# A fused attention and two-MLP kernel: weight operands combined on VectorE a step ahead, later stream loads, deferred results in pieces

## The chip, the cores and the metric

One core of one Trainium2 chip runs the whole program. The metric is the device time of one execution in microseconds. TensorE (PE) multiplies matrices, ScalarE (ACT), VectorE (DVE) and GpSimd (POOL) work elementwise, and SyncE (SP) only issues transfers. Each engine works through its own instructions in their order and waits at each for what that one needs.

## The reference

Attention in two steps (32 packed queries per head attend to 576 keys, then the 576 queries attend to the packed result), an RMS norm with a gated MLP (512 to 1536 to 512), and a second MLP (512 to 2048 to 512) with a leaky activation, in float32 for 4608 tokens.

```
p_packed = sm_attn(p, k, v)
x = sm_attn(q, p_packed, p_packed)              # 8 x 8 heads x 576 x 64 -> 4608 x 512
xn = x / rms * rms_g
x = (silu(xn @ w_gate) * (xn @ w_val)) @ w_out  # 512 -> 1536 -> 512
h = x @ w_in
out = (max(h, 0) + alpha * min(h, 0)) @ w_out2  # 512 -> 2048 -> 512
```

## The kernel before, in words

Every float32 product is made of three products of halves: an operand is split into a high half on ScalarE (`split_hi`, L110) and the rest as a low half by a subtraction (`split_lo` on VectorE, L113), and `mm3` (L122 to L124) multiplies high by high, high by low and low by high.

**Stage one** does the attention and the gated MLP in 12 chunks of 320 or 512 tokens (`CH`, the loop over it begins at L938). A chunk has 12 steps `f`; a step multiplies into the two input banks, makes `s` (tanh on ScalarE, two VectorE operations), splits it, and multiplies the result of the step before by a block of `w_out`. Beside it, the generator `conv_late` prepares the weights of the second MLP in chunks 1 to 10. The last chunk (320 tokens) has no attention beside it; there `prep` makes the operands of the first pair of stage two, and `making` (below) its output weights.

**Stage two** is the second MLP, seven products in place of eight (the Winograd form of Strassen's scheme) for a two by two split, in five pairs of token blocks (`PAIRS`: 512, 512, 512, 384, 384 tokens each half). A pair has a loop over `i` = 0 to 7 and then 40 later blocks (`LATER`). An iteration of the loop makes seven products of a weight block with an operand half (`prod`, six matmuls each) into three PSUM banks `a`, `b_`, `c_`; VectorE adds them up (`m1` copied by ScalarE at L1224, then `u2`, `u3`, `h22`, `h12`, `h21`, `s1`, `s2`, `s3`), ScalarE and VectorE do the leaky activation (`halves_of`, `prelu`), and two output blocks of an earlier iteration are put between (`fill`). The product `prod(b_, 6)` writes on in the bank that `u2` reads, so it waits for `u2`.

**Weight operands.** Each weight needs seven combined blocks per `i`; `sevenths` makes them from four blocks of 128 x 256: `product` splits one (high on ScalarE, low on GpSimd at L288) into a buffer named `w7o` of which there are two, and SP stores it to `w7_dram` or `o7_dram`; `combine` (L292, GpSimd) adds or subtracts blocks in place. A set is made in four steps with 2, 1, 1 and 3 products and the sums between them. For the input weights the steps run in stage one, for the output weights in `make_o7`: a step that loads a 512 KB block (`o_raw`, L276), then the four steps. `next(making)` is called once per `f` in the last chunk and five times per iteration of the first pair (`make(pr)`).

**Stream.** All 560 combined blocks are read back in order of use into 12 buffers (`load_next`, L926): one load at each `f` of the last chunk, then one after each block's use. A load waits for its buffer's last reader, and every transfer in SP's row behind it waits too.

Of the kernel before, what the change touches and what calls it, by code (L numbers as in the profile page):

```python
# [18 lines left out]
def attention_moe_moe2_kernel(ctx, tc, q, k, v, p, w_gate, w_val, w_out, rms_g, w_in2, w_out2, alpha, out):  # L19
    nc = tc.nc  # L20
# [105 lines left out]
    with tc.manual_schedule():  # L126
# [146 lines left out]
        def make_o7():  # L273
            for i in range(NP2):
                t = one.tile([128, 2, 512], F32, tag="w64", name="o2_raw", bufs=NST)
                nc.sync.dma_start(out=t, in_=w_dram[i])  # L276
                yield
                yield from sevenths("o2", i, [t[:, e] for e in range(2)])

        def sevenths(kind, i, pair):  # L280
# [4 lines left out]
            def product(n, src):  # L285
                t = one.tile([128, 2, 256], F32R, tag="w7o", name="w7o", bufs=2)
                split_hi(t[:, 0], src)
                nc.gpsimd.tensor_tensor(out=t[:, 1], in0=src, in1=t[:, 0].bitcast(F32), op=ALU.subtract)  # L288
                nc.sync.dma_start(out=kept[i * 7 + n], in_=t.bitcast(F32))
# [4 lines left out]
            product(0, b11)  # L294
            product(3 if kind == "i2" else 2, b22)
            yield
            if kind == "i2":
                product(1, b12)
                combine(b22, b21, b22, ALU.add)
                yield  # L300
                combine(b21, b11, b21)
                product(4, b22)
                combine(b11, b22, b11)
                yield
                product(6, b21)
                combine(b12, b12, b11)
                product(5, b11)
                product(2, b12)
            else:
                product(1, b21)  # L310
                combine(b11, b12, b11)
                yield
                combine(b12, b22, b12)
                product(4, b11)
# [583 lines left out]
        LATER = [(x, n, i) for x, n in (("b", 5), ("c", 2), ("b", 6), ("d", 3), ("a", 1)) for i in range(NP2)]  # L898
        LAG = 2

        def all_blocks():
            q = [None, None]
            for pr in range(len(PAIRS)):
                for i in range(NP2):
# [4 lines left out]
                    q += [("o", i, 0), ("o", i, 4)]  # L909
# [28 lines left out]
        for c, (t0, n, cuts) in enumerate(CH):  # L938
# [100 lines left out]
            for f in range(NF):  # L1039
# [9 lines left out]
                if last:  # L1049
# [9 lines left out]
                    load_next()  # L1059
# [111 lines left out]

        acc = {}

        def make(pr):
            if pr == 0:
# [30 lines left out]
        for pr, (t0, w) in enumerate(PAIRS):  # L1206
            final = pr + 1 == len(PAIRS)
            late_h, waiting = {}, []
            for i in range(NP2):
# [10 lines left out]
                make(pr)  # L1220
# [10 lines left out]
                make(pr)  # L1231
# [11 lines left out]
                make(pr)  # L1243
# [4 lines left out]
                for _ in block("a", 0, i, g11, w, i == 0, i == NP2 - 1):  # L1248
# [3 lines left out]
                make(pr)  # L1252
# [10 lines left out]
                make(pr)  # L1263
# [5 lines left out]
            for f_ in waiting:  # L1269
                f_()  # L1270
            m1s, m5s, u2s, u3s = {}, {}, {}, {}

            def copies(to, x, w=w):
                for j, m in pieces(w):
                    to[j] = temp(m)
                    evac(to[j], banks(x, j)[:, 0:m], True)

            def sums(to, x, m1s=m1s, w=w):
                for j, m in pieces(w):
                    to[j] = temp(m)  # L1280
                    add2(to[j], m1s[j], banks(x, j)[:, 0:m])

            def results(r0, half, put, w=w, end=False):
                stg = one.tile([128, TPC, 256], F32, tag="w64", name="stg2", bufs=NST)
                rows = out[r0:r0 + w, half * 256:(half + 1) * 256].rearrange("(n p) d -> p n d", p=128)
                for j, m in pieces(w):
                    put(stg.rearrange("p n d -> p (n d)")[:, j * T:j * T + m], j, m)
                    n = m // 256
                    if end:
                        nc.sync.dma_start(out=rows[:, 2 * j:2 * j + n], in_=stg[:, 2 * j:2 * j + n])  # L1290
                if not end:
                    nc.sync.dma_start(out=rows, in_=stg[:, 0:w // 128])

            def done_a(final, t0=t0, w=w):
                results(t0, 0, lambda o, j, m: evac(o, banks("a", j)[:, 0:m], j == 0 or not final), w, final)
# [88 lines left out]
```

## Time and profile before

| | us |
|---|---|
| median of 3 runs | 1734.27 (1730.31 to 1735.71) |
| profiled execution | 1731.16 |
| its span | 1729.4 |
| busy: TensorE, VectorE, ScalarE, GpSimd | 1594.4, 1143.1, 898.7, 345.8 |

The profiled execution's time is its span and 1.8 us around it. Busy time of TensorE is not TensorE at its best rate: matmuls overlap, and the clock granted to it changes. The stretch from about 880 to 1070 us is the one in which the page's slices show TensorE at 5 to 8 tenths with the clock under full; everywhere else after the start it is at 9.

### The profile page before, as it was taken

The page shows a single profiled execution, that of the slowest core. Times are in us where ns is not written, and L with a number is a line of the kernel's source. Part 1 is how long each engine was busy: PE and PEld are TensorE (multiplying, and loading weights), DVE is VectorE, ACT ScalarE, POOL GpSimd, SP SyncE. Part 2 cuts the span into 40 slices and gives each one's busy share as a digit, 9 for nine tenths or more (in the row PEclk, how much of TensorE's full clock was granted, in tenths as well). Part 3 has the DMA queues.
Part 4 walks back from the last instruction along what each step waited for, and adds up shares of the span by engine and source line. Part 5 has one row for each costly group of instructions (what it writes and reads, how often), then busy time and mean ns, then how long its engine had stood idle before and what let it go on. Part 6 is the DMA issues. An engine that isn't in the chain of part 4 may idle for free.

```text
span 1729.4 us, 32037 instructions
## 1 busy us (share of the span) xinstructions
PE 1594.4 (92%) x11786; PEld 1397.7 (81%) x11786; DVE 1143.1 (66%) x2132; ACT 898.7 (52%) x1906; POOL 345.8 (20%) x350
## 2 busy tenths in 40 slices
PE   7789999999999999999988557999999999999999
PEld 5457887887878878788877446898899889999999
DVE  4786656656566565666445445877787778688776
ACT  4556455554555544555444334545565555555554
POOL 1441243334343412122123332000000000000000
PEclk8899999999999999999999878999999999999999
DMA  9876555546655656645355666576767667888876
GB/s 241 253 240 203 152 175 169 136 125 187 188 162 178 189 176 214 228 151 193 107 205 209 209 205 221 172 245 204 214 206 223 191 199 225 256 265 258 264 230 199
DMA packets 233884, 348.95 MB, mean 202 GB/s; under 512 B 62848, under 2 KB 96640, under 8 KB 233728
## 3 DMA queue, kind: packets, MB, share of 16 engines
q1 hardware_dynamic: 233728, 346.90, 64.8%
q8 instruction: 94, 1.54, 0.4%
q14 instruction: 62, 0.51, 0.1%
HBM read 284.96 MB, written 61.87 MB: 201 GB/s over the span
## 4 chain that ended last, share of the span: by engine, by line
PE 62%; DVE 12%; issue 8%; DMA 7%; ACT 6%; POOL 4%; SPq 1%; POOLq 0%; ACTq 0%; DVEq 0%
PE ps_g L122 10%; PE ps_g L123 10%; PE ps_g L124 10%; PE ps_y L122 7%; PE ps_y L124 7%; PE ps_y L123 6%; DMA o_raw<-w_dram 3%; PE ps_wg L744 2%; DVE hl L113 2%; POOL w7o L288 2%; PE ps_v L122 2%; PE ps_v L123 2%; PE ps_v L124 2%; DMA o_dram<-w7o 1%; DVE kept L1148 1%
## 5 line engine op out<-in xcount | busy, mean ns | idle before, releaser
L122 PE MATMUL ps_g<-yh,w 128*128 128x512 f32 (+1 forms) x560 | 211.6, 378 | 49.1 <-DVE tmp L1145 49.1
L122 PE MATMUL ps_y<-hh,in_h 128*128 128x320 f32 (+1 forms) x576 | 209.4, 364 | 13.9 <-ACT hh L110 13.9
L123 PE MATMUL ps_g<-yl,w 128*128 128x512 f32 (+1 forms) x560 | 209.7, 375 | 0.0
L124 PE MATMUL ps_g<-yh,w 128*128 128x512 f32 (+1 forms) x560 | 208.7, 373 | 0.0
L123 PE MATMUL ps_y<-hl,in_h 128*128 128x320 f32 (+1 forms) x576 | 199.0, 345 | 3.8 <-DVE hl L113 3.0
L124 PE MATMUL ps_y<-hh,in_l 128*128 128x320 f32 (+1 forms) x576 | 197.6, 343 | 1.5 <-DMA in_l<-lo_dram 1.5
L1068 DVE SCALAR_TENSOR_TENSOR s<-s,ps_g 128x320 f32<-128x320 f32 (+1 forms) x132 | 71.4, 541 | 159.1 <-ACT s L1063 158.9
L124 PE MATMUL ps_y<-w,hl 128*128 128x256 f32 x576 | 164.2, 285 | 8.7 <-DVE hl L113 8.5
L110 ACT ACTIVATE hh<-kept 128x512 fp32r<-128x512 f32 (+1 forms) x200 | 116.9, 588 | 106.1 <-PE ps_g L123 51.6
L122 PEld LDWEIGHTS ps_y<-hh,in_h 128*128 128x128 f32 x576 | 110.4, 192 | 67.7 <-issue 42.2
L122 PE MATMUL ps_y<-w,hh 128*128 128x256 f32 x576 | 163.0, 283 | 1.9 <-ACT hh L110 1.9
L123 PE MATMUL ps_y<-w,hh 128*128 128x256 f32 x576 | 162.8, 283 | 0.0
L122 PEld LDWEIGHTS ps_g<-yh,w 128*128 128x128 f32 x560 | 107.6, 192 | 64.4 <-DVE tmp L1145 52.1
L110 ACT ACTIVATE hh<-s 128x320 fp32r<-128x320 f32 (+1 forms) x144 | 75.6, 525 | 160.2 <-DVE s L1072 160.0
L1145 DVE TENSOR_TENSOR tmp<-tmp,ps_g 128x512 f32<-128x512 f32 (+2 forms) x140 | 87.9, 632 | 96.6 <-PE ps_g L124 58.0
L113 DVE TENSOR_TENSOR hl<-kept,hh 128x512 fp32r<-128x512 f32 (+1 forms) x200 | 121.0, 632 | 18.4 <-ACT hh L110 18.0
L113 DVE TENSOR_TENSOR hl<-s,hh 128x320 fp32r<-128x320 f32 (+1 forms) x144 | 85.9, 597 | 60.6 <-ACT hh L110 60.6
L375 POOL TENSOR_TENSOR in_l<-w_raw,in_h 128x512 fp32r<-128x512 f32 x72 | 94.1, 1307 | 157.6 <-ACT in_h L110 130.9
L124 PE MATMUL ps_g<-w,hl 128*128 128x256 f32 x432 | 123.3, 286 | 1.4 <-DVE hl L113 1.3
L122 PE MATMUL ps_g<-xh,wgh 128*128 128x256 f32 (+3 forms) x352 | 114.4, 325 | 10.5 <-DVE s L1068 3.2
L122 PE MATMUL ps_g<-w,hh 128*128 128x256 f32 x432 | 122.9, 284 | 0.0
L123 PE MATMUL ps_g<-w,hh 128*128 128x256 f32 x432 | 122.9, 284 | 0.0
(196 smaller groups left out, 4278.3 us busy)
## 6 DMA issues: line engine op xcount, KB each, us to landing
w<-w_dram SPq DMA_DIRECT2D x280, 256.0 KB, 3.0
w<-o_dram SPq DMA_DIRECT2D x280, 256.0 KB, 2.9
gv_raw<-gv_dram SPq DMA_DIRECT2D x168, 256.0 KB, 3.9
in_l<-lo_dram SPq DMA_DIRECT2D x59, 256.0 KB, 3.4
w<-in_moe_w_out_dram SPq DMA_DIRECT2D x28, 512.0 KB, 5.1
w_dram<-w7o SPq DMA_DIRECT2D x56, 256.0 KB, 2.4
o_dram<-w7o SPq DMA_DIRECT2D x56, 256.0 KB, 2.0
vt<-in_v_dram SPq DMA_DIRECT2D x16, 576.0 KB, 5.3
```

Of the source, the lines that this page charges most:

```text
L110: nc.scalar.activation(out=hi, in_=src, func=ACTF.Copy)
L113: nc.vector.tensor_tensor(out=lo, in0=src, in1=hi.bitcast(F32), op=ALU.subtract)
L122: nc.tensor.matmul(out=o, lhsT=lh, rhs=rh, start=first, stop=False, skip_group_check=more)
L123: nc.tensor.matmul(out=o, lhsT=lh, rhs=rl, start=False, stop=False, skip_group_check=more)
L124: nc.tensor.matmul(out=o, lhsT=ll, rhs=rh, start=False, stop=last, skip_group_check=more)
L288: nc.gpsimd.tensor_tensor(out=t[:, 1], in0=src, in1=t[:, 0].bitcast(F32), op=ALU.subtract)
L375: nc.gpsimd.tensor_tensor(out=l, in0=raw[u], in1=h.bitcast(F32), op=ALU.subtract)
L744: nc.tensor.matmul(out=ts[g][h * NP:(h + 1) * NP, :], lhsT=ppG[b][e * D:(e + 1) * D, c_, :], rhs=us[c_][e * D:(e + 1) * D, :], start=True, ...
L1068: nc.vector.scalar_tensor_tensor(out=s, in0=s, scalar=1.0, in1=tg, op0=ALU.add, op1=ALU.mult)
L1145: nc.vector.tensor_tensor(out=out, in0=x, in1=y, op=ALU.add)
L1148: nc.vector.tensor_tensor(out=out, in0=x, in1=y, op=ALU.subtract)
```

## The change

- `sevenths`: the low half of a product and the sums move from GpSimd to VectorE, a step has at most two products, and a block is summed in the step before its product. The four steps have 2, 1, 2, 2 products for both weights (with 0, 2, 2, 0 sums).
- `make_o7`: the load of the next `o_raw` is issued in the second of the four steps, so there is no step of its own; 33 steps in place of 40. `make` is called three times per iteration, and not for `i` = 7.
- In stage two the `w7o` buffers alternate between two tags, four buffers in all (the tag `w32` is free in the first pair's loop).
- `load_next` is not called in the first three `f` of the last chunk, so each later load goes into a buffer freed three blocks earlier.
- `LATER` has 41 blocks: the last `c`,4 block stands third in it. The results (`sums`, `results`) are generators of which a step runs one piece (`one_after`), `copies` runs right behind its block, and `prepare` runs at odd steps when no piece waits.

```diff
         def make_o7():
+            ahead = [raw_pair(0)]
+            yield
             for i in range(NP2):
+                t = ahead.pop(0)
+                for n, _ in enumerate(sevenths("o2", i, [t[:, e] for e in range(2)])):
+                    if n == 1 and i + 1 < NP2:
+                        ahead.append(raw_pair(i + 1))
+                    yield
...
-                nc.gpsimd.tensor_tensor(out=t[:, 1], in0=src, in1=t[:, 0].bitcast(F32), op=ALU.subtract)
+                    t = one.tile([128, 2, 256], F32R, tag=tags[0], name="w7o", bufs=2)
+                    tags.append(tags.pop(0))
+                    split_hi(t[:, 0], src)
+                    split_lo(t[:, 1], src, t[:, 0])
...
-                nc.gpsimd.tensor_tensor(out=out, in0=x, in1=y, op=op)
+                nc.vector.tensor_tensor(out=out, in0=x, in1=y, op=op)
...
-                product(6, b12)
-                combine(b21, b21, b22)
-                product(5, b22)
-                product(3, b21)
+                products((0, b11), (2, b22))
+                yield
+                products((1, b21))
+                combine(b11, b12, b11)
+                combine(b12, b22, b12)
                 yield
+                products((4, b11), (6, b12))
+                combine(b22, b22, b11)
+                combine(b21, b21, b22)
+                yield
+                products((5, b22), (3, b21))
...
+        LATER.insert(2, ("c", 4, NP2 - 1))
...
                     next(making)
-                    load_next()
+                    if f > 2:
+                        load_next()
...
+        seventh_tags[0] = ["w7o", "w32"]
...
-        def make(pr):
-            if pr == 0:
+        def make(pr, i):
+            if pr == 0 and i < NP2 - 1:
                 next(making, None)
...
-                if (k_ + 1) * 3 // 8 > k_ * 3 // 8:
+                if after:
+                    one_after()
+                elif k_ % 2:
                     next(prepare, None)
```

ScalarE in the last chunk, around the step with three products; `w7o<-o_raw` are the high halves, `s<-ps_g` the tanh of the next `f`. Before:

```order
L110 ACTIVATE yh<-y_raw 128x512
L110 ACTIVATE w7o<-o_raw 128x256 x3
L1063 ACTIVATE s<-ps_g 128x320
L110 ACTIVATE hh<-s 128x320
L110 ACTIVATE in_h<-w_raw 128x512
L110 ACTIVATE yh<-y_raw 128x512
L1063 ACTIVATE s<-ps_g 128x320
```

The same place now:

```order
L110 ACTIVATE yh<-y_raw 128x512
L110 ACTIVATE w7o<-o_raw 128x256 x2
L1075 ACTIVATE s<-ps_g 128x320
L110 ACTIVATE hh<-s 128x320
L110 ACTIVATE in_h<-w_raw 128x512
L110 ACTIVATE yh<-y_raw 128x512
L110 ACTIVATE w7o<-o_raw 128x256 x2
L1075 ACTIVATE s<-ps_g 128x320
```

The third high half no longer stands in the row of the first two, and the step that only loaded is gone, so the next set begins one `f` earlier.

SP in the loop of the first pair, around the load of `o_raw`; `o_dram<-w7o` are the stores, `w_...` the stream loads. Before:

```order
L289 DMA o_dram<-w7o 128x512 x3
L926 DMA w_11781<-o_dram 128x512
L926 DMA w_11789<-w_dram 128x512
L926 DMA w_11806<-w_dram 128x512
L276 DMA o_raw<-w_dram 128x1024
L289 DMA o_dram<-w7o 128x512 x2
```

Now:

```order
L302 DMA o_dram<-w7o 128x512
L276 DMA o_raw<-w_dram 128x1024
L937 DMA w_11923<-o_dram 128x512
L937 DMA w_11931<-w_dram 128x512
L937 DMA w_11948<-w_dram 128x512
L302 DMA o_dram<-w7o 128x512 x2
```

Before, the load stood right ahead of the two stores of products made from it; now the stores behind it are of the set before it, and its own products come three steps, one iteration, later.

VectorE in the loop of the first pair, from the activation of `h22` to `s3` (`kept<-neg` is that activation, `tmp<-tmp,ps_g` is `h12`, `kept<-tmp,ps_g` is `h21`). Before:

```order
L1157 SCALAR_TENSOR_TENSOR kept<-neg,alpha_sb,kept 128x512
L1145 TENSOR_TENSOR tmp<-tmp,ps_g 128x512
L113 TENSOR_TENSOR hl<-tmp,hh 128x512
L1145 TENSOR_TENSOR kept<-tmp,ps_g 128x512
L1157 SCALAR_TENSOR_TENSOR tmp<-neg,alpha_sb,tmp 128x512
L1145 TENSOR_TENSOR tmp<-tmp,kept 128x512
L1148 TENSOR_TENSOR kept<-tmp 128x512 x2
```

Now, in an iteration whose three steps are the third, the fourth and the first of a set:

```order
L1169 SCALAR_TENSOR_TENSOR kept<-neg,alpha_sb,kept 128x512
L113 TENSOR_TENSOR w7o<-o_raw,w7o 128x256 x2
L1157 TENSOR_TENSOR tmp<-tmp,ps_g 128x512
L113 TENSOR_TENSOR hl<-tmp,hh 128x512
L113 TENSOR_TENSOR w7o<-o_raw,w7o 128x256 x2
L1157 TENSOR_TENSOR kept<-tmp,ps_g 128x512
L1169 SCALAR_TENSOR_TENSOR tmp<-neg,alpha_sb,tmp 128x512
L1157 TENSOR_TENSOR tmp<-tmp,kept 128x512
L1160 TENSOR_TENSOR kept<-tmp 128x512 x2
```

Two groups of low halves stand in VectorE's row, ahead of `h12` and ahead of `h21`; a third stands ahead of `u3`.

## Rows read from the trace of the kernel before

**Rows 1.** Busy time by stretch: stretch, length, busy us per engine, TensorE clock, DMA share, GB/s.
```profile
872.60:936.10 63.50, 49.87 (x273) 46.59 (x272) 31.95 (x57) 29.14 (x66) 19.17 (x24) 0.89 0.64 224
936.10:1083.90 147.80, 98.67 (x462) 81.95 (x461) 68.65 (x98) 59.45 (x121) 51.14 (x66) 0.83 0.63 213
...
1096.60:1244.40 147.80, 145.66 (x937) 133.02 (x938) 114.72 (x178) 78.74 (x136) 0.00 (x0) 1.00 0.70 212
```
**Rows 2.** ScalarE in order of time: start, length, the copy of `m1`.
```profile
938.10 0.58 ACT L1224 ACTIVATE tmp<-ps_g 128x512 f32<-128x512 f32 x1
...
1083.92 0.60 ACT L1224 ACTIVATE tmp<-ps_g 128x512 f32<-128x512 f32 x1 [0.80 <-PE ps_g L124]
1157.37 0.60 ACT L1224 ACTIVATE tmp<-ps_g 128x512 f32<-128x512 f32 x1 [3.18 <-PE ps_g L124]
...
1244.45 0.60 ACT L1224 ACTIVATE tmp<-ps_g 128x512 f32<-128x512 f32 x1 [0.80 <-PE ps_g L124]
```
**Rows 3.** Waits of TensorE, 936.1 to 1083.9: total us, times, longest.
```profile
PE ps_g L122 <- DVE tmp L1145: 49.1, 7, 10.0
```
**Rows 4.** Waits of ScalarE, 936.1 to 1083.9.
```profile
ACT w7o L110 <- DMA o_dram<-w7o: 30.0, 12, 2.9
...
ACT w7o L110 <- DMA o_raw<-w_dram: 22.8, 5, 5.2
```
**Rows 5.** All engines in order of time, 998.3 to 1008.4, first pair's loop.
```profile
998.33 0.42 SPq L276 DMA_DIRECT2D o_raw<-w_dram  x1
...
1003.28 0.72 ACT L110 ACTIVATE w7o<-o_raw 128x256 fp32r<-128x256 f32 x2 [4.58 <-DMA o_raw<-w_dram]
...
1006.64 0.42 ACT L110 ACTIVATE w7o<-o_raw 128x256 fp32r<-128x256 f32 x1 [2.63 <-DMA o_dram<-w7o]
...
1008.31 0.79 PE L122 MATMUL ps_g<-yh,w 128*128 128x512 f32 x1 [9.44 <-DVE tmp L1145]
```
**Rows 6.** Tile `w7o`: count, shortest, median and longest ns, first and last start.
```profile
L110 ACT ACTIVATE w7o<-o_raw x56: 399/416/420, 881.4 to 1066.5; 128x256 fp32r<-128x256 f32 x56
```
**Rows 7.** VectorE by form, 870 to 940: busy us, mean ns.
```profile
L113 DVE TENSOR_TENSOR xl<-A2T,xh 128x128 fp32r<-128x128 f32 x1 | 0.3, 293 | 0.7 <-ACT xh L110 0.7
```
**Rows 8.** VectorE by form, 936.1 to 1083.9, GpSimd at work.
```profile
L113 DVE TENSOR_TENSOR hl<-tmp,hh 128x512 fp32r<-128x512 f32 x13 | 12.3, 947 | 18.5 <-ACT hh L110 18.5
```
**Rows 9.** VectorE by form, 1096.6 to 1244.4, GpSimd idle.
```profile
L113 DVE TENSOR_TENSOR hl<-tmp,hh 128x512 fp32r<-128x512 f32 x14 | 9.6, 685 | 0.0
```
**Rows 10.** VectorE in order of time, `hl`, `h21`, `s2` with `s3`; second pair's loop.
```profile
1253.46 0.69 DVE L113 TENSOR_TENSOR hl<-tmp,hh 128x512 fp32r<-128x512 f32 x1
1254.07 0.69 DVE L1145 TENSOR_TENSOR kept<-tmp,ps_g 128x512 f32<-128x512 f32 x1
...
1256.42 1.29 DVE L1148 TENSOR_TENSOR kept<-tmp 128x512 f32<-128x512 f32 x2
```
**Rows 11.** TensorE in order of time, last chunk, undisturbed.
```profile
878.40 0.31 PE L122 MATMUL ps_g<-xh,wgh 128*128 128x320 f32 x1
...
880.01 0.31 PE L124 MATMUL ps_v<-xh,wgl 128*128 128x320 f32 x1
```
**Rows 12.** Waits of ScalarE, 872.6 to 936.1.
```profile
ACT w7o L110 <- DMA o_dram<-w7o: 6.9, 2, 4.0
ACT w7o L110 <- DMA o_raw<-w_dram: 6.5, 2, 4.4
```
**Rows 13.** Waits of ScalarE, 240 to 860.
```profile
ACT w7o L110 <- DMA w_dram<-w7o: 26.6, 9, 4.2
```
**Rows 14.** TensorE in order of time, stops behind those waits, first and last.
```profile
265.84 1.30 PE L451 MATMUL ps_at<-kT,pT 64*32 64x288 f32 x16 [0.56 <-DVE s L1068]
...
761.70 0.42 PE L122 MATMUL ps_g<-xh,wgh 128*128 128x320 f32 x1 [3.16 <-DVE s L1068]
```
**Rows 15.** TensorE in order of time, first of the later blocks, second pair.
```profile
1259.03 0.39 PE L124 MATMUL ps_y<-w,hl 128*128 128x256 f32 x1 [1.43 <-DVE hl L113]
```
**Rows 16.** Tile `w`, all its transfers: shortest, median and longest us to landing.
```profile
DMA to landing us min/median/max: 2.0/3.0/10.2
```

More of the change, by code (lines that the diff above doesn't have):

```diff
@@ L273, in make_o7, with raw_pair @@
         def make_o7():
[L274 removed]
+            def raw_pair(i):
                 t = one.tile([128, 2, 512], F32, tag="w64", name="o2_raw", bufs=NST)
                 nc.sync.dma_start(out=t, in_=w_dram[i])
[L277 to L278 removed]
+                return t
+            ahead = [raw_pair(0)]
+            yield
+            for i in range(NP2):
+                t = ahead.pop(0)
[3 more added lines that the diff above has]
+                    yield
+        seventh_tags = [["w7o"]]
         def sevenths(kind, i, pair):
@@ L283, in sevenths, with products @@
             kept = w7_dram if kind == "i2" else o7_dram
-            def product(n, src):
-                t = one.tile([128, 2, 256], F32R, tag="w7o", name="w7o", bufs=2)
-                split_hi(t[:, 0], src)
-                nc.gpsimd.tensor_tensor(out=t[:, 1], in0=src, in1=t[:, 0].bitcast(F32), op=ALU.subtract)
-                nc.sync.dma_start(out=kept[i * 7 + n], in_=t.bitcast(F32))
+            def products(*which):
+                for n, src in which:
+                    tags = seventh_tags[0]
+                    t = one.tile([128, 2, 256], F32R, tag=tags[0], name="w7o", bufs=2)
+                    tags.append(tags.pop(0))
+                    split_hi(t[:, 0], src)
+                    split_lo(t[:, 1], src, t[:, 0])
+                    nc.sync.dma_start(out=kept[i * 7 + n], in_=t.bitcast(F32))
@@ L1208, in attention_moe_moe2_kernel, with copies @@
             late_h, waiting = {}, []
+            m1s, m5s, u2s, u3s = {}, {}, {}, {}
+            def copies(to, x, w=w):
+                for j, m in pieces(w):
+                    to[j] = temp(m)
+                    evac(to[j], banks(x, j)[:, 0:m], True)
             for i in range(NP2):
@@ L1247, in attention_moe_moe2_kernel @@
                 add2(h12, u2, c_)
-                for _ in block("a", 0, i, g11, w, i == 0, i == NP2 - 1):
+                then = (lambda f_=copies, to=m1s: f_(to, "a")) if i == NP2 - 1 else None
+                for _ in block("a", 0, i, g11, w, i == 0, i == NP2 - 1, then):
                     pass
@@ L1268, in attention_moe_moe2_kernel @@
                 ]
[L1269 to L1276, printed above, removed]
+            waiting[0]()
             def sums(to, x, m1s=m1s, w=w):
@@ new lines, in done_a, with done_b6, done_c @@
+            def done_a(final=final, t0=t0, w=w, results=results, taken=taken):
+                x = taken("a")
+                for _ in results(t0, 0, lambda o, j, m: evac(o, x[j][:, 0:m], j == 0 or not final), w, final):
+                    pass
+            def done_b6():
+                after.append(sums(u2s, [banks("b", j) for j, _ in pieces(w)]))
+            def done_c():
+                x = taken("c")
+                after.append(results(t0, 1, lambda o, j, m: add2(o, u2s[j], x[j][:, 0:m])))
@@ new lines, in done_b7, with done_d, one_after @@
+            def done_b7():
+                after.append(sums(u3s, taken("b")))
+                after.append(results(t0 + w, 1, lambda o, j, m: add2(o, u3s[j], m5s[j])))
+            def done_d():
+                x = taken("d")
+                after.append(results(t0 + w, 0, lambda o, j, m: add2(o, u3s[j], x[j][:, 0:m])))
+            after = []
+            def one_after():
+                while after:
+                    if next(after[0], after) is not after:
+                        return
+                    after.pop(0)
@@ L1348, in attention_moe_moe2_kernel @@
                 pass
+            while after:
+                one_after()
             while len(fill) > 2:
```

66 lines of the change are left out of this document (21 added, 45 removed).

## The prediction

> **What bounds the kernel now.** I read the page's slices first, then the busy time by stretch, then who waits for whom in the stretch that stands out. TensorE is nearly always busy; the exception begins with the last chunk. Two stretches of the same length do the same kind of loop: the first pair's (936.1 to 1083.9) has 98.7 us of TensorE work at a granted clock of 0.83, the second pair's has 145.7 at 1.00 [rows 1]. The copy of `m1`, once per iteration, is a clean ruler: seven iterations take 1083.92 - 938.10 = 145.8 us in the first pair and 1244.45 - 1157.37 = 87.1 in the second, 20.8 against 12.44 each [rows 2]. So 58.7 us are lost there. TensorE's waits are 49.1 of it, all one kind: `prod(b_, 6)` waits for `u2` on VectorE [rows 3]. VectorE is not the cause, it waits for the copy of `m1`, and ScalarE cannot copy because a high half stands ahead of it. One case shows it: SP issues the load of `o_raw` at 998.33; ScalarE starts the halves at 1003.28 after 4.58 us idle for that load, then waits 2.63 for the store that frees a `w7o` buffer, starts the third half at 1006.64, and TensorE goes on at 1008.31 after 9.44 idle [rows 5]. In total ScalarE waits 22.8 us for `o_raw` and 30.0 for the stores [rows 4]. Most of the other 9.6 us are the matmuls at the low clock after each stop.
>
> **The change part by part.** The sum is made against the profiled execution: span 1729.4, 1731.2 with what lies around it, 3 below the median of the runs (the table ahead).
>
> *First pair's loop, waits removed.* `o_raw` is now issued three steps, an iteration, ahead of its use; landing takes about 5 us [rows 5], an iteration over 12. The buffers are four and a step takes two, so a buffer's store has a step between, some 4 us, where the third half above came 3.4 us after the first two and had waited for it. Both waits go. What is late next is the chain VectorE to ScalarE to VectorE. The cost added: 21 steps over seven iterations, 11 operations of 128 x 256 per four steps, 8.25 per iteration. The form isn't in the trace; between 293 ns for 128 columns [rows 7] and 685 for 512 [rows 9] lies 424 by a straight line, and since VectorE starts its next operation before the last has ended (0.61 between the starts of two of 0.69 [rows 10]), 0.34 on the path: 2.8 us per iteration, 0.92 per step. VectorE's own work in that loop is 14 operations by 0.61, 8.6 us of 12.4, so the sum fits; the order costs more than the sum. One step's low halves stand ahead of `h21`, and their high halves stand on ScalarE behind the two activations of `h12`. From the start of `h12`: VectorE is done with `hl` after 1.2; ScalarE needs 0.7 for `h12`, 1.2 for two activations, 0.42 for the first half [rows 6], so the low halves begin at 2.3 and end at 3.2. `h21` to `s3` take 3.5 (1254.07 to 1257.7, less a short gap [rows 10]), to 6.7. Then `u2`, the activation of `h21`, `hl` and a step: 0.7 + 0.7 + 0.6 + 0.9, to 9.6. `prod(b_, 6)` began at 7.5 when `u2` was done, `prod(a, 1)` ends 2.8 later at 10.3, ScalarE's and VectorE's activations behind it take to 13.4, and the third step 0.9: the next `h12` starts at 14.3. So 14.3 us per iteration, 1.9 over TensorE's own 12.4, the loop 100: **46 us gained**. The bounds: 12.44, the cover is complete (58.7 gained), and 16.5, each of the three steps idles like the worst one (30).
>
> *GpSimd out of the way.* With GpSimd at work the same `hl` took 947 ns on average, without it 685 [rows 8, 9]. This helps VectorE by 13 x 0.26 = 3.4 us, already in the 0.34 and the 14.3, since they come from rows without GpSimd. The Trainium skill, SBUF — State Buffer, section "Who interferes with whom", says that a two-input VectorE operation with both inputs in SBUF contends with GpSimd's reads, and that the later one is blocked whole; the trace agrees, 947 against 685 ns [rows 8, 9]. By that rule alone the sum would be 3.4 us better than with VectorE's speed as it was in that loop; the sum above holds without it.
>
> *Last chunk.* 872.6 to 936.1; TensorE needs 24 products per `f` at (880.01 - 878.40) / 11 = 0.146 us [rows 11], 3.5 us, 38.7 for the 264 that stand there before the first pair. ScalarE waits 6.9 for stores and 6.5 for `o_raw` [rows 12]; the first `o_raw` wait, about 2, stays, since it is issued at the start as before. 11 us go. Added on VectorE: 31 operations by 0.34, 10.5 us, while it is idle 63.5 - 31.95 = 31.5 [rows 1]. Bounds: 1 if all is on the path, 14 if none is and the clock recovers; I take 8, nearer to the idle row.
>
> *Stage one.* ScalarE waits 26.6 us in nine pieces for a store [rows 13], the third product in one step; now a step has two, and its buffers were stored a step or more before. What of it TensorE feels is less: nine stops of TensorE follow right behind those waits, from 0.56 at 265.84 to 3.16 at 761.70, 12.4 us together [rows 14]. Against it 88 operations by 0.34 = 30 us go onto VectorE, most into gaps while it waits for the tanh. Bounds -5 and +14, I take **6**.
>
> *Stream loads.* A load no longer waits for the block just issued, so it no longer holds the stores behind it; the lead falls from twelve blocks to nine, 9 x 1.4 = 12.6 us, against a landing of 3.0, at most 10.2 [rows 16]. Nothing, as long as that lead covers it (the last rival is what it costs if not).
>
> *Later blocks.* Each pair's later blocks start with a stop of 1.43 us [rows 15], waiting for the low half of the last `c`,4 block. That block goes two places back, but the block put in its place has its own low half at the same place in VectorE's row, behind `s3` and the activation of `h21`: zero. The pieces spread VectorE's work but don't lessen it. I take **1**, bounds -4 and +7 (all five stops go).
>
> Sum: 46 + 8 + 6 + 1 = 61; 1731.2 - 61 = 1670.
>
> **The rivals.** *Complete cover:* VectorE runs ahead far enough that TensorE sets the pace in the loop, and every stop behind a store goes: 58.7 + 14 + 12 + 5 = 90, **1641**. For it: 8.6 + 2.8 us of VectorE in 12.4. Against: the row order above, with a wait for ScalarE inside. 0.16.
>
> *VectorE becomes the bound:* every one of the three steps idles 1 us for its halves as the worst one does, 16.5 per iteration (gain 30), and the last chunk and stage one gain nothing since the 40 us put on VectorE stand between `s` and its split: 1731 - 30 + 3 = **1704**. For it: VectorE is the engine that TensorE's own wait names [rows 3]. The Trainium skill, Perfetto Trace Analysis, "Optimizing Scalar/DVE Operations", speaks against the change here: work should go off a saturated VectorE, perhaps to GpSimd, though it warns that this may not help as the two share a read port. In the trace VectorE is busy 114.7 of 147.8 us in the second pair [rows 1], high but not full. 0.12.
>
> *It doesn't do what it says:* a load of `o_raw` waits for a `w64` buffer held by a row store, or the store is late, and half the waits of ScalarE stay: 1731 - 26 - 4 = **1701**. The rotation of the four buffers shows every earlier holder done before. 0.04.
>
> *Slower, late loads:* the nine-block lead doesn't cover the landing once the first pair's loop also stores 1.4 MB and reads 0.4 MB more per iteration than the second's, 4.1 MB in 14.3 us (290 GB/s, where 212 is 0.70 of the engines [rows 1]), and in all five pairs each block then waits for its weights. It decides at a landing of 12.6 us; the 61 us are eaten when each of the 560 blocks waits 0.11 us, and at 0.14 the time is **1748**. Against: 3.0 median, 10.2 the worst [rows 16]. 0.03.
>
> **How the numbers follow.** The forecast, 1670, has 0.65; its own range by the bounds is 1652 to 1692. The range reaches to complete cover and stops short of the VectorE bound and the two below it: 1640 to 1696, 0.19 left out. Faster by over 0.3%, about what a measurement of this kernel can tell from no change, holds in all cases but the last: 0.95; the last has most of the rest, 0.03 slower and 0.02 within.
>
> **What would show it.** Right: ScalarE's waits of `w7o` for `o_raw` and for stores are near zero in the first pair's loop; the copies of `m1` stand 13 to 15 us apart; TensorE's wait for `u2` is 1 to 3 us each, not 9.5; the granted clock there is near 1.00; the second to fourth pairs stay at 160 us. Wrong: copies over 16 us apart with VectorE busy through; `o_raw` waits still there; stops of TensorE at a block with a stream load as the cause; or later blocks whose stops have grown.

## The result, and the profile after

The changed kernel takes 1677.9 us (median of 4 runs, 1677.7 to 1682.3) against 1734.1 for the kernel before beside it: ratio 0.9685, 95% interval 0.9663 to 0.9707. A control, the same kernel again in another set of runs, gave 0.9695 (0.9666 to 0.9724). One execution of that control, its profiled one, ran at a granted clock of 0.652 from end to end (2152.6 us) and is left out of every comparison.

The page of the changed kernel, busy time of each engine and TensorE's slices (the dip at 880 to 1070 us is nearly gone):

```profile
PE 1587.7 (94%) x11786; PEld 1391.8 (83%) x11786; DVE 1198.7 (71%) x2308; ACT 894.5 (53%) x1906; POOL 206.3 (12%) x174
PE   7789999999999999999997988999999999999999
PEclk8799999999999999999999999999999999999999
```

The stretches that answer to [rows 1]: last chunk, then the seven iterations of the first pair's loop (columns as there).

```profile
868.90:932.00 63.10, 49.46 (x281) 44.79 (x281) 41.48 (x88) 30.02 (x70) 0.00 (x0) 0.95 0.71 240
932.00:1035.20 103.20, 93.47 (x466) 77.93 (x464) 82.50 (x153) 56.24 (x118) 0.00 (x0) 0.97 0.83 287
```

The stretch of [rows 1] begins 2.0 us ahead of the first copy of `m1`. From that copy to the eighth the loop fell from 145.8 to 103.2 us, its clock rose from 0.82 to 0.97, and VectorE's work in it grew from 67.7 to 82.5. The ruler, the copies of `m1` on ScalarE (first, two in the middle, last), answers to [rows 2]:

```profile
932.02 0.58 ACT L1243 ACTIVATE tmp<-ps_g 128x512 f32<-128x512 f32 x1
...
974.42 0.58 ACT L1243 ACTIVATE tmp<-ps_g 128x512 f32<-128x512 f32 x1
991.03 0.58 ACT L1243 ACTIVATE tmp<-ps_g 128x512 f32<-128x512 f32 x1
...
1035.24 0.58 ACT L1243 ACTIVATE tmp<-ps_g 128x512 f32<-128x512 f32 x1
```

1035.24 - 932.02 = 103.2, so 14.75 us per iteration, with the longest 16.6 from 974 to 991. The waits in that loop, of TensorE, ScalarE and VectorE in turn (total us, times, longest):

```profile
PE ps_g L122 <- DVE tmp L1157: 9.7, 7, 2.3
```

```profile
ACT neg L1164 <- DVE kept L1157: 10.2, 7, 1.9
ACT neg L1164 <- DVE tmp L1157: 9.0, 7, 1.7
...
ACT w7o L110 <- DMA o_dram<-w7o: 1.3, 1, 1.3
```

```profile
DVE w7o L113 <- ACT w7o L110: 8.5, 8, 1.1
```

TensorE's wait for `u2` fell from 49.1 to 9.7 [rows 3], ScalarE's for stores from 30.0 to 1.3, and its 22.8 for `o_raw` are gone [rows 4]. ScalarE's waits for VectorE grew from 2.6 to 19.2, and new is VectorE's for a product's high half (8.5): seven of its eight pieces, 1.06 to 1.08 us each, stand at the step ahead of `h21`, one per iteration. From the last `m1` of that loop to the end nothing changed: 1729.4 - 1083.92 = 645.5 before [rows 2], 1680.5 - 1035.24 = 645.3 now.

The experiments below are read by the same rulers: stage one from the row copies (`stg`) at the end of its second chunk to those of its eleventh, the last chunk from there to the first `m1`, the loop from the first `m1` to the eighth. All in us, each from one profile; medians are of all runs of a set.

| kernel | median | ratio (95%) | stage one | last chunk | loop |
|---|---|---|---|---|---|
| before | 1731 to 1734 | 1 | 630.5 | 67.3 | 145.8 |
| changed | 1677.9 | 0.9685 (0.9663-0.9707) | 628.6 | 64.9 | 103.2 |
| e1: GpSimd again | 1649.6 | 0.9518 (0.9495-0.9542) | 614.4 | 59.7 | 90.6 |
| e2: load at use | 1706.8 | 0.9848 (0.9824-0.9872) | 625.4 | 69.7 | 125.9 |
| e3: two buffers | 1679.8 | 0.9695 (0.9668-0.9722) | 626.3 | 63.7 | 104.3 |
| e4: stream loads early | 1676.8 | 0.9684 (0.9665-0.9702) | 626.3 | 63.2 | 101.7 |
| e5: old later blocks | 1679.6 | 0.9698 (0.9676-0.9719) | 629.1 | 62.8 | 101.6 |
| e6: before, two edits | 1695.2 | 0.9793 (0.9765-0.9821) | 634.3 | 66.5 | 109.9 |
| e7: one step moved | 1669.1 | 0.9637 (0.9615-0.9658) | 626.8 | 63.9 | 92.8 |
| e9: low halves a step later | 1667.0 | 0.9628 (0.9609-0.9647) | 629.2 | 58.5 | 95.3 |
| e10: e1, more buffers | 1649.6 | 0.9524 (0.9497-0.9551) | 615.0 | 57.3 | 91.1 |
| e11: only low halves on GpSimd | 1659.3 | 0.9588 (0.9557-0.9619) | 618.1 | 63.8 | 92.4 |
| e12: e10, first block early | 1640.2 | 0.9472 (0.9459-0.9485) | 615.7 | 58.6 | 91.1 |

Seven profiles have stage one as changed; they spread from 625.4 to 629.2; the two with stage one as before (before, e6) lie 3.8 apart, the three with GpSimd (e1, e10, e12) 1.3. So a difference under 4 us in that column says nothing. The changed kernel's profile was of the longest of its four runs, 4.4 over the median.

### The profile page after: what moved, and what is told of

Same layout as the page of the kernel before. It is cut to its first block, busy times and chain, and to the rows that moved or that the text cites. A ratio compares the mean times of both kernels' runs of the same rounds, so it can differ in the third digit from the quotient of the medians.

```text
span 1680.5 us, 31955 instructions
## 1 busy us (share of the span) xinstructions
PE 1587.7 (94%) x11786; PEld 1391.8 (83%) x11786; DVE 1198.7 (71%) x2308; ACT 894.5 (53%) x1906; POOL 206.3 (12%) x174
## 4 chain that ended last, share of the span: by engine, by line
PE 67%; DVE 17%; ACT 8%; DMA 4%; issue 3%; SPq 1%; POOL 0%; DVEq 0%; ACTq 0%; POOLq 0%
PE ps_g L122 11%; PE ps_g L124 10%; PE ps_g L123 10%; PE ps_y L122 8%; PE ps_y L123 7%; PE ps_y L124 7%; PE ps_wg L754 3%; DVE hl L113 2%; PE ps_v L122 2%; PE ps_v L123 2%; PE ps_v L124 2%; ACT hh L110 1%; DVE s L1084 1%; DMA o_dram<-w7o 1%; DVE w7o L113 1%
## 5 line engine op out<-in xcount | busy, mean ns | idle before, releaser
L122 PE MATMUL ps_g<-yh,w 128*128 128x512 f32 (+1 forms) x560 | 209.5, 374 | 12.4 <-DVE tmp L1157 11.5
L113 DVE TENSOR_TENSOR hl<-s,hh 128x320 fp32r<-128x320 f32 (+1 forms) x144 | 82.1, 570 | 60.7 <-ACT hh L110 60.7
L1157 DVE TENSOR_TENSOR tmp<-tmp,ps_g 128x512 f32<-128x512 f32 (+2 forms) x140 | 88.2, 630 | 49.1 <-PE ps_g L124 48.6
L123 PEld LDWEIGHTS ps_y<-hl,in_h 128*128 128x128 f32 x576 | 110.6, 192 | 13.0 <-DVE hl L113 6.5
```

The costliest lines, as they stand in the source:

```text
L113: nc.vector.tensor_tensor(out=lo, in0=src, in1=hi.bitcast(F32), op=ALU.subtract)
L122: nc.tensor.matmul(out=o, lhsT=lh, rhs=rh, start=first, stop=False, skip_group_check=more)
L123: nc.tensor.matmul(out=o, lhsT=lh, rhs=rl, start=False, stop=False, skip_group_check=more)
L1157: nc.vector.tensor_tensor(out=out, in0=x, in1=y, op=ALU.add)
```

## The experiments

The theory is the prediction's: the loop's gain comes from ScalarE, no longer held by the load of `o_raw` and by stores; what remains is the chain through VectorE's row. Rivals: the gain comes from taking GpSimd out of VectorE's way, from SP's row, or from the later blocks.

### Which part carries the gain: e0 to e3

**e0**, the control:

> The changed kernel once more, as the control for the kernels run beside it. Both theories expect 1678 us (1674 to 1683) and a loop of the first pair of 14.3 to 15.0 us per iteration. If the profile of this run lies near 1678 rather than 1682, the difference shows where the 4.5 us of the profiled execution of the first set went.

Measured: 1680.4, ratio 0.9695, as the first set; for where the changed kernel's time lies e3 and e4 serve, which take the same time.

**e1**, only the engine undone:

```diff
-                    split_lo(t[:, 1], src, t[:, 0])
+                    nc.gpsimd.tensor_tensor(out=t[:, 1], in0=src, in1=t[:, 0].bitcast(F32), op=ALU.subtract)
...
-                nc.vector.tensor_tensor(out=out, in0=x, in1=y, op=op)
+                nc.gpsimd.tensor_tensor(out=out, in0=x, in1=y, op=op)
```

> Only the engine is undone: low halves and sums on GpSimd again, all else as changed. Theory (the gain comes from ScalarE no longer being held by the load of o_raw and by stores): the gain stays. GpSimd has room (51 of 148 us in that loop before), VectorE's row loses 8.25 operations per iteration (-2 us each iteration, the chain ahead of h21 becomes shorter) and VectorE is slowed where GpSimd reads (+3.4 us in the loop): 1668 to 1684 us. Rival (the gain comes from taking GpSimd out of VectorE's way): most of the 43 us of the loop are lost, 1700 us or more, copies of m1 17 us or more apart.

Measured: 1649.6, 28 to 31 us *shorter* than the changed kernel (1677.9 and, beside it, 1680.4). The rival falls, and the theory's bound was not low enough either: the part of the change that stands first in its name costs some 29 us. Profile against profile, the changed kernel's being 4.4 over its median, it is 33.6: 14 in stage one, 5 in the last chunk, 12.6 in the loop, the rest ahead of and behind these. TensorE's and GpSimd's waits in the loop of e1:

```profile
PE ps_g L122 <- DVE tmp L1157: 2.2, 4, 0.8
```

```profile
POOL w7o L301 <- ACT w7o L110: 29.2, 15, 4.3
```

GpSimd waits 29 us for high halves, and nobody waits for it there; in the changed kernel VectorE does that waiting, with `h21` and `u2` behind it. The price that the move was to save is real, and it doesn't decide. VectorE by form in the loop of e1 (busy us, mean ns | idle before):

```profile
L1157 DVE TENSOR_TENSOR tmp<-tmp,ps_g 128x512 f32<-128x512 f32 x21 | 14.3, 679 | 1.9 <-PE ps_g L124 1.8
L1160 DVE TENSOR_TENSOR kept<-tmp 128x512 f32<-128x512 f32 x13 | 13.6, 1080 | 0.2
L113 DVE TENSOR_TENSOR hl<-tmp,hh 128x512 fp32r<-128x512 f32 x13 | 12.6, 969 | 0.0
```

and the same three in the changed kernel:

```profile
L1157 DVE TENSOR_TENSOR tmp<-tmp,ps_g 128x512 f32<-128x512 f32 x21 | 14.3, 681 | 1.9 <-PE ps_g L124 1.5 <-ACT tmp L1243 0.4
...
L113 DVE TENSOR_TENSOR hl<-tmp,hh 128x512 fp32r<-128x512 f32 x13 | 8.9, 683 | 0.0
L1160 DVE TENSOR_TENSOR kept<-tmp 128x512 f32<-128x512 f32 x13 | 8.4, 688 | 0.2
```

Beside GpSimd the last two forms took 8.9 us longer (26.2 against 17.3), yet the loop was 12.6 us shorter.

**e2**, only the load ahead undone:

```diff
-            ahead = [raw_pair(0)]
             yield
             for i in range(NP2):
-                t = ahead.pop(0)
-                for n, _ in enumerate(sevenths("o2", i, [t[:, e] for e in range(2)])):
-                    if n == 1 and i + 1 < NP2:
-                        ahead.append(raw_pair(i + 1))
-                    yield
+                t = raw_pair(i)
+                yield from sevenths("o2", i, [t[:, e] for e in range(2)])
```

> Only the load ahead is undone: o_raw is loaded in the step that uses it. Theory (ScalarE held by the load): five loads in the seven iterations of the first pair's loop, ScalarE waits 4 to 5 us for each, 20 to 25 us in all, of which VectorE's slack hides a little; TensorE loses 15 to 25 us there and 2 to 5 in the last chunk: 1695 to 1708 us. Rival (GpSimd out of the way, or SP's row): 1676 to 1684 us, since neither changes.

Measured: 1706.8, 26 to 29 us longer, the loop 125.9, 23 of it. The theory holds. ScalarE's waits in the loop, then one case in order of time:

```profile
ACT w7o L110 <- DMA o_raw<-w_dram: 19.3, 5, 5.7
```

```profile
967.62 0.72 ACT L110 ACTIVATE w7o<-o_raw 128x256 fp32r<-128x256 f32 x2 [5.54 <-DMA o_raw<-w_dram]
968.06 0.76 DVE L113 TENSOR_TENSOR w7o<-o_raw,w7o 128x256 fp32r<-128x256 f32 x2 [6.72 <-ACT w7o L110]
```

ScalarE's 5.5 us become 6.7 of VectorE, since the low halves stand in its row.

**e3**, only the buffers undone:

```diff
-        seventh_tags[0] = ["w7o", "w32"]
+        seventh_tags[0] = ["w7o"]
```

> Only the buffers are undone: two for the products in the first pair's loop, still at most two products per step. Theory as the prediction has it (the waits for stores go because a buffer's store has a step between): with two buffers a step's halves wait for the stores of the step before; halves, low halves and the landing of a store take about 1 + 1 + 2.5 us against 4.9 us between steps, so the waits are short: 0 to 12 us longer, 1678 to 1690. Rival (the third product alone was the trouble, two per step need no more buffers): 1677 to 1680. Second rival (buffers carry the store's part of the gain whole): 20 to 25 us longer, 1700.

Measured: 1679.8, the same as the control. ScalarE's waits for stores in the loop are 3.7 us in six pieces, 2.4 more than with four, and the loop is 1 us longer than the changed kernel's, 2.6 longer than those of e4 and e5, which have four buffers too. The total doesn't show it: with two products per step, two buffers do.

### What the old layout of steps costs: e6

The kernel before with the load ahead and four buffers, nothing else:

```diff
+                    if n == 1 and i + 1 < NP2:
+                        ahead.append(raw_pair(i + 1))
...
-                t = one.tile([128, 2, 256], F32R, tag="w7o", name="w7o", bufs=2)
+                tags = seventh_tags[0]
+                t = one.tile([128, 2, 256], F32R, tag=tags[0], name="w7o", bufs=2)
+                tags.append(tags.pop(0))
...
+        seventh_tags[0] = ["w7o", "w32"]
```

> The kernel before with two edits alone: o_raw loaded a set's second step ahead of its use (without a step of its own), and four buffers for the products in stage two. Steps with three products, GpSimd, the stream loads and the later blocks as before. Theory (in the first pair's loop ScalarE's two waits are all there is, and four buffers cover a third product): the loop 90 to 96 us in place of 146, the last chunk 2 to 5 us less, stage one unchanged: 1672 to 1684. Rival (the third product in a step keeps ScalarE waiting for stores, four buffers or not): the loop 105 us or more, 1690 or more.

Measured: 1695.2, the loop 109.9. The gain, 36 us, is all in the loop, 14 to 20 less of it than the theory wanted. The rival's numbers came, but not for its reason. ScalarE's waits there, and one case:

```profile
ACT w7o L110 <- POOL o_raw L304: 16.1, 12, 3.0
ACT neg L1164 <- DVE tmp L1157: 4.5, 6, 1.1
ACT w7o L110 <- DMA o_dram<-w7o: 4.1, 2, 3.1
```

```profile
991.82 0.42 ACT L110 ACTIVATE w7o<-o_raw 128x256 fp32r<-128x256 f32 x1 [2.98 <-POOL o_raw L304]
```

With the load and the stores out of the way ScalarE waits for a *sum* that GpSimd makes in the same step. This wait was 3.6 us in the kernel before, small beside the two in [rows 4], which had covered it. With the sum made a step ahead of its product, still on GpSimd, it is 4.3 us (e1). From e6 to e1, which differ by the steps' layout (and how often one runs) and by two parts that e4 and e5 find worth nothing, 45.6 us go, 19.3 in the loop, 16 to 20 in stage one, 6.8 in the last chunk. In these last two it is the waits for stores that fall, from 27.9 us (e6) to 7.1 (e1) between 240 and 850 us and from 13.6 to 5.1 in the last chunk: there the layout helps because no step has a third product. In the loop the pace differs too. With five steps per iteration e6 is done with them early in the fifth iteration; the first four take 16.8 to 18.2 us, the last two 12.44, while e1 spreads them over seven of 12.2 to 13.7; no run separates the pace from the sum made ahead. So of the changed kernel's edits the layout of the steps and the load ahead carry the gain, some 82 us in all with GpSimd kept.

### What VectorE's part costs in the loop: e7, e9, e11

**e7** moves the step that stands ahead of `h21` behind `s3`:

```diff
-                make(pr, i)
                 h21 = keep(1, i, w)
...
                 less2(s3, g11, h12)
+                make(pr, i)
```

> The step that stands ahead of h21 is moved behind s3, to the iteration's end. Theory (the chain: its low halves wait for high halves that stand behind two activations, with h21 and all behind it in VectorE's row): the copies of m1 come 13.2 to 13.8 us apart in place of 14.8, the loop 93 to 97 us, 1667 to 1672 in all. First rival (VectorE's busy time sets the pace, not the order): the loop stays at 102 to 105 us, 1677 to 1682. Second rival (the low halves now stand ahead of the next u2, so that prod(b_, 6) waits as long as h21 did): also 1677 to 1682, with TensorE waiting 2 us for u2.

Measured: 1669.1; copies of `m1` from 928.50 to 1021.34, 13.26 us apart, inside the range worked out from the chain. TensorE's wait for `u2` is 3.6 us in four pieces, clock 1.00, and the wait for high halves is gone from VectorE's list of waits, though it does the same work, in stretches of 94 and 104 us:

```profile
928.00:1022.00 94.00, 90.15 (x465) 75.66 (x464) 82.65 (x154) 57.06 (x120) 0.00 (x0) 1.00 0.88 308
```

```profile
932.00:1036.00 104.00, 93.83 (x466) 77.93 (x464) 83.27 (x154) 57.04 (x120) 0.00 (x0) 0.97 0.83 287
```

The first is e7, the second the changed kernel: VectorE 82.7 and 83.3 us busy, 154 operations each. It is the place in the row, not the work. (The edit moves the step's high halves in ScalarE's row as well; e9, which leaves them where they are, separates the two rows.)

**e9** issues the low halves and the store one step after the high halves, with more product buffers in the last chunk:

```diff
-                    split_lo(t[:, 1], src, t[:, 0])
-                    nc.sync.dma_start(out=kept[i * 7 + n], in_=t.bitcast(F32))
+                    lows.append((t, src, i * 7 + n))
+                    if kind == "i2":
+                        finish()
...
+                finish()
                 products((4, b11), (6, b12))
...
+                        seventh_tags[0] = ["w7o", "gv"]
```

> The low halves stay on VectorE but are issued one step after their high halves, in the last chunk and the first pair's loop, so that VectorE's row never stands waiting for a high half just issued; in the last chunk the products have more buffers (the ones that stage two uses for its temporaries), without which the later low halves would hold them. Stage one as changed. The run before showed that the same operations on GpSimd give 13 us less in the loop, 4 in the last chunk and 12 in stage one. Theory (in the loop it is the waiting in VectorE's row): the loop 90 to 95 us, the last chunk 2 to 6 us less, 1660 to 1670 in all. Rival (it is VectorE's busy time, 8 operations more per iteration): the loop 100 to 105, 1674 to 1681.

Measured: 1667.0, the loop 95.3, the last chunk 58.5, 6.4 less. Again the work is the same, and only VectorE's part of it has another place. (How much of the last chunk's 6.4 is due to the buffers isn't shown.) ScalarE waits for stores again, and the products are stored a step later; that this eats some of the loop's gain is argued, not shown.

```profile
ACT w7o L110 <- DMA o_dram<-w7o: 12.1, 13, 2.9
```

**e11** puts the low halves on GpSimd and leaves the sums on VectorE:

```diff
-                    split_lo(t[:, 1], src, t[:, 0])
+                    nc.gpsimd.tensor_tensor(out=t[:, 1], in0=src, in1=t[:, 0].bitcast(F32), op=ALU.subtract)
```

> The changed kernel with only the low halves back on GpSimd, the sums stay on VectorE. Theory (what VectorE's part costs is the low halves, which wait in its row for a high half just issued; sums wait for nothing): most of the 28 us that GpSimd gave come back, the loop of the first pair 90 to 94 us, stage one within 4 us of that run, 1648 to 1657. Rival (it is the number of operations put on VectorE, of which sums are 64 of 176): about two thirds of the 28 us come back, 1658 to 1663, with the loop at 94 to 97.

Measured: 1659.3, a split verdict. The loop, 92.4, is as the theory has it; the total is the rival's, since the last chunk keeps 4 us of the price and stage one about as much (3.7, near what that column can tell). ScalarE's wait for `s` in the last chunk, in e1 and then with only the sums on VectorE (e11), shows where it comes from:

```profile
ACT hh L110 <- DVE s L1084: 15.6, 12, 2.2
```

```profile
ACT hh L110 <- DVE s L1084: 21.0, 12, 3.0
```

In the changed kernel it is 22.3. So there the sums, which wait for nothing, carry most of the price, since they stand between `s` and its split. Whether their number or their place counts no run tells.

### The parts held to be worth nothing: e4, e5

```diff
-                    if f > 2:
-                        load_next()
+                    load_next()
```

> Only the lead of the stream loads is undone: a load is issued at every f of the last chunk, so that each load of stage two again waits for the block just issued and SP's row stands behind it. Theory (the distance of the stream loads is worth nothing, since nine blocks and twelve both cover a landing of 3 us, and stores behind a waiting load come at most 1 to 2 us later, with two or four buffers for them): 1676 to 1684 us, as the changed kernel. Rival (the stores held in SP's row were a large part of ScalarE's waits): 1688 us or more, with waits of ScalarE for stores back in the first pair's loop.

Measured: 1676.8, nothing. SP's waits for a block before a stream load grow from 3.4 us to 8.1 between 870 and 1030; ScalarE doesn't wait for a store in the loop, and in the last chunk its one wait is 3.8 us (5.7 in the changed kernel).

e5 takes back the later blocks as a whole:

```diff
-        LATER.insert(2, ("c", 4, NP2 - 1))
...
-                if after:
-                    one_after()
-                elif k_ % 2:
+                if (k_ + 1) * 3 // 8 > k_ * 3 // 8:
                     next(prepare, None)
```

> Only the later blocks are undone: the last c,4 block where it stood, results and copies in one go. Theory (the five stops at the start of the later blocks stay whichever block stands there, and the pieces lessen no work): 1675 to 1684 us, the time from the last copy of m1 in the first pair to the end 645 us as before and after. Rival (the pieces and the moved block gave 5 us or more, which the profile hid among other differences): 1685 us or more.

Measured: 1679.6, nothing either: with the buffers of e3, three of the five parts of the change can't be measured.

### Going on from e1: e10, e12

**e10** is e1 with the buffers that stage two uses for its temporaries lent to the products in the last chunk:

```diff
+                        seventh_tags[0] = ["w7o", "gv"]
...
-                    t = one.tile([128, 2, 256], F32R, tag=tags[0], name="w7o", bufs=2)
+                    t = one.tile([128, 2, 256], F32R, tag=tags[0], name="w7o", bufs=8 if tags[0] == "gv" else 2)
```

> The changed kernel with low halves and sums on GpSimd, as in the run that gave 1650, and in the last chunk more buffers for the products (the ones that stage two uses for its temporaries). Theory (of the 5.1 us that ScalarE still waits for stores in that chunk TensorE feels one stop of 4.2): 2 to 5 us less than that run, 1645 to 1648. Rival (the stop is hidden or comes back as a wait for o_raw or y_raw): 1648 to 1651.

Inconclusive: the profile is 2.9 us shorter than e1's (1644.0 against 1646.9), 2.4 of it in the last chunk, and the medians are equal. ScalarE's 5.1 us of waits for stores are gone there, and TensorE's wait for ScalarE falls from 7.3 to 4.8 us, but a wait for a load of `in_l` stands in its place; both lines are e10's:

```profile
PE ps_y L122 <- ACT hh L110: 4.8, 3, 4.4
PE ps_y L124 <- DMA in_l<-lo_dram: 3.0, 2, 2.5
```

**e12** adds to e10 that the halves of the first later block are issued in the last iteration:

```diff
+                if i == NP2 - 1:
+                    early = block("b", 5, 0, late_h[0][2], w, True, False)
+                    next(early)
                 n12 = halves_of(h12, h12, w)
...
+                if i == NP2 - 1:
+                    next(early)
                 h21 = keep(1, i, w)
...
-            next(splits[0])
```

> As the run with GpSimd and more buffers in the last chunk (1650, its profiled execution 1646), and in each pair the high and low half of the first later block (b,5,0) are issued within the last iteration, ahead of h21, so that its low half no longer stands in VectorE's row behind s3 and the activation of h21. Theory (the five stops at the start of the later blocks, 8.4 us in that profile, come from that place in the row alone): the stops go, 5 to 8 us less, 1638 to 1645. Rival (the next block's low half is late in its place, or h21 is): the stops stay at 1 us or more each, 1646 to 1651.

Measured: 1640.2, the shortest of all, and 9 us below e10 by the ratios (0.9472 against 0.9524), of which the profiles show 4.7 (1639.3 against 1644.0; e10's profile was of its shortest run). From the eighth `m1` to the end it takes 635.8 us, where the profiles of all the other kernels lie between 642.0 and 646.9. TensorE's wait at the start of the later blocks, e10 from 1001 to the end, then e12:

```profile
PE ps_g L124 <- DVE hl L113: 8.4, 5, 1.9
```

```profile
PE ps_g L124 <- DVE hl L113: 4.4, 5, 1.0
```

Half of each stop goes; the theory said all. What is left is still a low half, 0.8 to 1.0 us each time, and it is the second block's: in the first pair the twelve matmuls of the first block start without a stop from 1015.35 to 1016.67, and the stop of 0.80 us is at the third matmul of the next twelve, at 1017.98.

## Why the prediction was right, and where not

The forecast was 1670 in a range of 1640 to 1696; 1677.9 came, and the likeliest case was the one that happened. Of its sum of 61 us the two profiles show 48.9 (1729.4 to 1680.5) and the medians 56.2; the profile of before was 3 us under its median, that of the changed kernel 4.4 over. Term by term:

*The loop*, 46 forecast, 42.6 measured: right, mechanism and size. Both waits of ScalarE went, the new bound is the chain through VectorE's row, 14.75 us per iteration against 14.3. The chain's idle time ahead of `h21`, 1.1 us in the forecast (from 1.2 to 2.3), was 1.06 to 1.08. e2 and e6 show that removing the waits carries the gain, e7 that the chain was read rightly: with that step out of its place the chain was forecast at 13.2 to 13.8, and 13.26 came. The missing 0.45, 3.1 us over the loop, is about what the clock cost in the iterations of 16.6 and 15.8 us (below); the forecast had it near 1.00 throughout. The four buffers, which the prediction gave part of the credit, are worth 1 to 2.6 us of the loop and nothing in the total (e3).

*The last chunk*, 8 forecast, 2.4 by the ruler (67.3 to 64.9) and 3.3 from the chunk's first product to the loop's first: the term that was mis-sized most. The step that failed is "11 us go": the waits for stores were taken to vanish, but one was left and grew. ScalarE, then TensorE in the changed kernel:

```profile
905.38 0.42 ACT L110 ACTIVATE w7o<-o_raw 128x256 fp32r<-128x256 f32 x1 [5.70 <-DMA o_dram<-w7o]
```

```profile
908.59 0.63 PE L122 MATMUL ps_y<-hh,in_h 128*128 128x320 f32 x1 [5.21 <-ACT hh L110]
```

The chunk has two buffers, and the stores of one step, issued together, are waited for by the next; in SP's row they come right behind two loads of `y_raw`. In e9 and e10, with more buffers, that wait is gone. So with GpSimd kept (e1) 7.6 us go in this chunk, and with more buffers too (e10) 10. The other part is the price on VectorE: 5.2 us (64.9 against e1's 59.7), where the forecast left 3 (11 less 8).

*Stage one*, 6 forecast, 1 to 9 measured (630.5 and 634.3 to between 625.4 and 629.2), inside its bounds. But it is a difference of two terms, both taken too small: e1 shows 16 us of relief or more (630.5 to 614.4) where 12.4 were forecast (the nine stops that were counted add up to 12.0 in the trace), and 11 to 15 us of price where the forecast left 6.4, "most into gaps while it waits for the tanh". That the errors cancel is luck. The step on the gaps failed, and in the last chunk too: an engine's idle time was counted without asking whether it lies where the operations stand. The rival in which VectorE's added work stands between `s` and its split was true in part, though its loop of 16.5 us was not: ScalarE's wait for `s` between 240 and 850 us is 106.2 us before, 107.1 in e1, 111.3 in e11 and 115.8 in the changed kernel, and in the last chunk it has the same order (e11).

*Stream loads* and *later blocks*, 0 and 1 forecast: nothing measured (e4, e5). The stop at the start of the later blocks that answers to [rows 15] (1.43, with 0.20 shortly before it) is still there, behind the same operation:

```profile
1212.37 0.39 PE L124 MATMUL ps_g<-w,hl 128*128 128x256 f32 x1 [1.86 <-DVE hl L113]
```

The forecast named VectorE's row as the reason, and e12, which changes that row, halves the stops.

*GpSimd out of the way*: 3.4 us were given to VectorE in the loop. That operations slow down beside GpSimd is confirmed. The Trainium skill, SBUF — State Buffer, "Who interferes with whom", says that a VectorE operation with two inputs in SBUF contends with GpSimd's reads and that one with at most one, outside the two-port modes, does not; the rows of e1 agree with both halves: 1080 against 688 ns and 969 against 683 for the forms with two, 679 against 681 for `tmp<-tmp,ps_g`, whose second input is in PSUM. But the prediction never asked what the kernel would do with the other edits and GpSimd kept. The Trainium skill, Perfetto Trace Analysis, "Optimizing Scalar/DVE Operations", which the prediction cited as speaking against the change, allows work to go from a saturated VectorE to GpSimd and doubts that it helps; here it did help, by some 29 us, with VectorE at 71% of the span.

*Late loads*: no stop of TensorE in the pairs has a stream load as its cause, at up to 325 GB/s in e12's loop.

## What to carry to other kernels

An operation added to an engine is priced by its place in that engine's row: if it waits there for another engine, everything behind it waits too, and the engine's idle share says nothing of that. An idle engine may do it at more than twice the time (1038 ns against 419 here) and with contention, and still win; where it must stay, issue it one step after what it waits for. When a wait is removed, look in the list for the small ones behind it (here a sum made in the step that uses it), since they are the next bound.

## What the runs showed of the hardware

Stops of about 2 us were followed by a low clock, not all of them. TensorE in the changed kernel's loop in order of time, and the same stretch by windows (the column behind the engines is the granted clock):

```profile
974.33 0.39 PE L124 MATMUL ps_g<-yh,w 128*128 128x512 f32 x1
976.55 0.65 PE L122 MATMUL ps_g<-yh,w 128*128 128x512 f32 x1 [1.84 <-DVE tmp L1157]
977.00 0.63 PE L123 MATMUL ps_g<-yl,w 128*128 128x512 f32 x1
...
980.30 0.39 PE L122 MATMUL ps_g<-yh,w 128*128 128x512 f32 x1
980.53 0.40 PE L123 MATMUL ps_g<-yl,w 128*128 128x512 f32 x1
```

```profile
970.00:974.70 4.70, 4.70 (x24) 3.65 (x22) 3.56 (x8) 3.33 (x7) 0.00 (x0) 1.00 0.99 336
976.50:980.30 3.80, 3.75 (x9) 2.93 (x10) 2.83 (x6) 0.00 (x0) 0.00 (x0) 0.55 0.74 260
```

Matmuls start 0.43 us apart for 3.8 us, near the lower of the clock's two levels (1.2 and 2.4 GHz), and 0.23 before and after: nine of them cost 1.7 us on top of the stop. The stop of 2.30 us that ended at 993.17 was followed by it too (0.50 from 994 to 997), the one of 1.49 at 1008.98 was not. The length alone doesn't decide: in e4 and e5 the same iteration has the same stop of 1.84 us and no low clock behind it, and takes 15.06 and 15.04 us in place of 16.61, while their stop of 2.29 us was followed by one. So the low clock cost 1.55 us there, nearly as much as the stop. In the loops of e1, e7 and e9, whose waits for `u2` are 1.4 us at most, the clock is 1.00.

GpSimd pays for the contention as well: its low half of 128 x 256 took 828 ns in the loop of the kernel before, where VectorE was busy 46% of the time, 927 in e6 (63% while the steps run) and 1038 in e1 (86%). Single operations look as if each had waited for the other whole. In the loop before, a `hl` that started at 985.45, beside a sum of GpSimd's that ended at 986.11, took 1.22 us in place of 0.69; the low half that GpSimd started at 986.07 ended at 987.25, 1.18 in place of 0.73. Waiting for the other's end and then running at full speed would put the two ends at 986.80 and 987.40, an estimate 0.13 and 0.15 us over what they were.
